# Five interleaved seven-product groups per chunk instead of three groups and six plain units, in a fused sliding-window attention and SwiGLU kernel

## The chip, the cores and the metric

One core of a Trainium2 chip. The metric is the device time of one launch in microseconds (us). The kernel before took 318.54 to 323.70 us over all rounds, a spread of 1.6%, so each kernel was run several times, in rounds that also ran the kernel before on the same chip. Some executions are in a slower state, with a lower granted clock. Four runs are marked so (two of run 2, one each of runs 3 and 7); the text says so there. All others, and all profiled ones, were fast.

## The reference, cut to what matters

```python
# q, k, v: (8 batches, 8 heads, 576, 64), fp32
scores = q @ k.T / 8, only where |i - j| <= 32
x = (softmax(scores) @ v) as 4608 tokens x 512
out = (silu(x @ w_gate) * (x @ w_val)) @ w_out      # 512 -> 1536 -> 512
```

The FFN is nearly all of the work. It is done in nine chunks of 512 tokens; the attention for chunk j + 1 runs among the FFN matmuls of chunk j. Chunk 0 is set-up. Chunks 1 to 6 carry attention, chunk 7 only the rest of it, chunk 8 none.

## The kernel before, the parts that matter

A *unit* computes 128 columns of h = silu(gate) * val plainly: eight matmuls of 512 columns, one ScalarE operation and one VectorE operation. A *group* computes 256 columns of h for the 512 tokens with seven products in place of eight (Winograd's form of a 2 x 2 block product): 28 matmuls of 256 columns. Around them ScalarE has five operations (three copies and two silu) and VectorE four (three sums and the product of silu and val). Matmuls write to PSUM, here in eight *banks*; to *drain* a bank is to read its result out with VectorE or ScalarE, after which it is free.

```python
def group_steps(j, f, xs, banks): ...   # one group; X, Y, Z are PSUM tiles
    "P1": X = wv(0).b11        "s1": keep X (ScalarE)
    "P2": Y = wv(1).b21        "c11": val = Y + s1 (VectorE)
    "P5": Z = s1w.xs[0]        "p5": keep Z
    "P6": X += s2w.xs[1]       "u2": keep X
    "P7": X += s3w.xs[2]       "c22": gate = X + p5 (VectorE)    "sc": silu(gate)
    "P3": Z += s4w.b22         "c12": val = Z + u2 (VectorE)
    "P4": X += wg(1).xs[3]     "sd": silu(X)                     "hm": h = silu * val
    # (shown in short; the signs are in the sums of weights and of x)
```

The order in which the steps are issued is a list, and each engine works through its own part of it in order (`pg`, `pv`: the gate and val halves of a unit; `As`, `Ds`, `Bs`: sums of h, which the second half needs). First half of a chunk before the change (`pg`, `pv`: the gate and val halves of a unit; `As`, `Ds`, `Bs`: sums of h, which the second half needs):

```python
pg0 pva0 pvm0 q0 k0 q1 t0
1P1 1s1 pvb0 1P2 1P5 1p5 1P6 1c11 1u2 pg1 ...
...
3P1 3s1 ... 3P7 3P3 3c22 m2 pvn3 3c12 3sc s3 3P4 m3 3sd
pg4 3hm pv4 s4 t6 m4 Bs0 flag pg5 pv5 s5 m5 Bs1 Bs2
```

Note the last line: after the last group's last product `3P4` two whole units follow, sixteen 512-column matmuls. The second half of a chunk (again seven products, now over h, here p1 to p7) with the attention of the next chunk in it:

```python
st["p1"](); st["s1"]()
...                                    # the rest of the sums of h, on VectorE
scores(0, ps_c); scores(1); scores(2)
exp(0); exp(1); exp(2)
st["p2"](); st["c11"]()                # c11: an output sum on VectorE
masked(0); masked(1); masked(2)        # VectorE
st["p6"](); st["u2"](); st["p5"](); st["k5"]()
av(0); av(1, ps_a); av(2, ps_a)        # attention x values
norm(0); norm(1); norm(2)              # VectorE; then the token transpose by DMA
st["p7"]() ...
```

The chain behind `norm` matters later: norm, DMA transpose of x into xT (the input of the next chunk's first matmul), and in the same queue the ten transposes of the q and k tokens that the scores half a chunk later need.

Of the kernel before, what the change touches and what calls it, by code (L numbers as in the profile page):

```python
# [132 lines left out]
def kernel(  # L133
# [29 lines left out]
    qk16 = fast.enter_context(tc.tile_pool(name="qk16", bufs=4))  # L163
    tkpool = fast.enter_context(tc.tile_pool(name="tk", bufs=18))
# [6 lines left out]
    ps_a = fast.enter_context(tc.tile_pool(name="ps_a", bufs=2, space=bass.MemoryType.PSUM))  # L171
    ps_c = fast.enter_context(tc.tile_pool(name="ps_c", bufs=1, space=bass.MemoryType.PSUM))
    ps_o = fast.enter_context(tc.tile_pool(name="ps_o", bufs=2, space=bass.MemoryType.PSUM))
# [102 lines left out]

    def cast_qk(st, cast):
        t16 = qk16.tile([128, J9, 2, D], FP16, tag="qk16", name="t16")
        cast(t16.rearrange("p j h d -> p h j d"),
             st.rearrange("p h (j d) -> p h j d", d=D))  # L280
        return t16
# [15 lines left out]


    xts = {}
# [24 lines left out]
    def pair_scores(m, pool=None, masked=True):  # L324
        s = (pool or ps_a).tile([128, 2, 8, 64], FP32, tag="c" if pool is ps_c else "a",
                                name="s_ps")
        for i in range(2):
            for g in range(HP):
                score_mms(s, 4 * i + g, m, i, g)
        p = pts[m] = ppool.tile([128, 2, 2, HP, 64], FP16, tag="p", name="p_t")  # L330
        ex = lambda: exp_act(p.rearrange("p e i g q -> p (e i g) q"),
                             s.rearrange("p e c q -> p (e c) q"))
        if not masked:
            return ex
        ex()
        pair_mask(m)

    def quad_scores(ms, F):

        if ms not in quads:  # L340
            quads[ms] = ppool.tile([128, 2, 2, 2, HP, 64], FP16, tag="p2", name="p2_t", bufs=2)
            for n, m in enumerate(ms):
                pts[m] = quads[ms][:, n]
# [19 lines left out]
    def pair_av(m, pool=None, normed=True):  # L363
# [3 lines left out]
        else:  # L367
            t2 = (pool or ps_c).tile([128, 2, 512], FP32, tag="a" if pool is ps_a else "c",
                                     name="o_ps")
# [30 lines left out]
    def turn_x(ms, pool, cast=None):  # L400
# [6 lines left out]
        if pool is None:  # L407
# [3 lines left out]
                       tag={ps_a: "a", ps_c: "c", ps_o: "o"}[pool], name="xt_ps")  # L411
# [4 lines left out]
        cast(dst.rearrange("p g (n t) -> p n g t", t=128), tp)  # L416
# [38 lines left out]
    def group_weights():  # L455

        s3 = qkst.tile([128, 3, 2, 768], FP16, tag="qkst", name="g_top")
        s4 = const.tile([128, 2, 768], FP16, name="g_rest")
        half = lambda w, k: w[:, 2 * k:2 * k + 2].rearrange(
            "p k (a c) -> p k a c", c=512)[:, :, :, 0:256]  # L460
        v0, v1, g0, g1 = half(wv16, 0), half(wv16, 1), half(wg16, 0), half(wg16, 1)
        gw["s"] = [s3[:, 0], s3[:, 1], s3[:, 2], s4]
        t1, t2, t3, t4 = [t.rearrange("p k (a c) -> p k a c", c=256) for t in gw["s"]]
        return [lambda k=k, o=o, a=a, b=b, op=op:
                nc.vector.tensor_tensor(out=o[:, k], in0=a[:, k], in1=b[:, k], op=op)
                for o, a, b, op in ((t1, g0, g1, ALU.add), (t2, t1, v0, ALU.subtract),
                                    (t3, v0, g0, ALU.subtract), (t4, v1, t2, ALU.subtract))
                for k in range(2)]

    def group_steps(j, i, xs, tiles):  # L470

        f = 2 * i
        x = xts[j]
        b11, b21, b22 = x[:, 0:2, 0:256], x[:, 2:4, 0:256], x[:, 2:4, 256:512]
        wv = lambda k: wv16[:, 2 * k:2 * k + 2, 512 * i:512 * i + 256]
        wg = lambda k: wg16[:, 2 * k:2 * k + 2, 512 * i:512 * i + 256]
        s1, s2, s3, s4 = [t[:, :, 256 * i:256 * i + 256] for t in gw["s"]]
        k = {}
        first = "ZX" if i == 2 else "X"

        def product(name, lhs, rhs, first):
            for n in range(2):
                for g in range(2):
                    nc.tensor.matmul(out=k[name][:, n], lhsT=lhs[:, g, 128 * n:128 * n + 128],  # L484
                                     rhs=rhs[:, g, :], start=(first and n == 0 and g == 0),
                                     stop=(g == 1), skip_group_check=True)

        def bank(name):
            pool = tiles[name]
            t = pool.tile([128, 2, 256], FP32, tag="c" if pool is ps_c else "o",  # L490
                          name=f"g{name}_ps")
            k[name] = t

        def keep_act(name, src):
            k[name] = opool.tile([128, 2, 256], FP32, tag="kept", name="kept", bufs=3)
            cast_act(k[name], k[src])

        def val(c, src, name):
            if "val" not in k:
                k["val"] = qk16.tile([128, 2, 512], FP16, tag="qk16", name="val")  # L500
            nc.vector.tensor_tensor(out=k["val"][:, :, 256 * c:256 * c + 256], in0=k[src],  # L501
                                    in1=k[name], op=ALU.add)
# [5 lines left out]
        def silu(c, src):  # L508
            if "silu" not in k:
                k["silu"] = qk16.tile([128, 2, 512], FP16, tag="qk16", name="silu")  # L510
            nc.scalar.activation(out=k["silu"][:, :, 256 * c:256 * c + 256], in_=k[src],  # L511
                                 func=AF.Silu, bias=0.0, scale=1.0)

        return {
            "P1": lambda: ([bank(n) for n in first], product("X", wv(0), b11, True)),
            "s1": lambda: keep_act("s1", "X"),
            "P2": lambda: (bank("Y"), product("Y", wv(1), b21, True)),
            "c11": lambda: val(0, "Y", "s1"),
            "P5": lambda: ("Z" in k or bank("Z"), product("Z", s1, xs[0], True)),
            "p5": lambda: keep_act("p5", "Z"),  # L520
            "P6": lambda: product("X", s2, xs[1], False),
            "u2": lambda: keep_act("u2", "X"),
            "P7": lambda: product("X", s3, xs[2], False),
            "c22": gate,
            "sc": lambda: silu(1, "gate"),
            "P3": lambda: product("Z", s4, b22, False),
            "c12": lambda: val(1, "Z", "u2"),
            "P4": lambda: product("X", wg(1), xs[3], False),
            "sd": lambda: silu(0, "X"),
            "hm": lambda: nc.vector.tensor_tensor(out=hts[j][:, 2 * f:2 * f + 2, :],  # L530
                                                  in0=k["silu"], in1=k["val"], op=ALU.mult),
        }

    def x_sums(j, eng):

        x = xts[j]
        b11, b12 = x[:, 0:2, 0:256], x[:, 0:2, 256:512]
        b21, b22 = x[:, 2:4, 0:256], x[:, 2:4, 256:512]
        t = ppool.tile([128, 4, 2, 256], FP16, tag="p2", name="x_sums", bufs=2)
        t1, t2, t3, t4 = [t[:, n] for n in range(4)]  # L540
        for o, a, b in ((t1, b12, b11), (t2, b22, t1), (t3, b22, b12), (t4, b21, t2)):
            eng.tensor_tensor(out=o, in0=a, in1=b, op=ALU.subtract)  # L542
        return t1, t2, t3, t4

    def unit_steps(j, fk):
# [3 lines left out]
        def half(i, w, parts=None):  # L549
            if i == 0:  # L550
                k["gv"] = ps_a.tile([128, 2, 512], FP32, tag="a", name="gv_ps")
            for g, c in parts or [(g, slice(0, 512)) for g in range(GS)]:
                nc.tensor.matmul(out=k["gv"][:, i, c], lhsT=w[:, g, 128 * fk:128 * fk + 128],  # L553
                                 rhs=xts[j][:, g, c], start=(g == 0 and c.start == 0),
                                 stop=(g == GS - 1), skip_group_check=True)

        def silu():
            k["s"] = spool.tile([128, 512], FP16, tag="s", name="ssb")
            nc.scalar.activation(out=k["s"], in_=k["gv"][:, 0, :], func=AF.Silu, bias=0.0,  # L559
                                 scale=1.0)  # L560

        first, second = [(0, slice(0, 256))], [(0, slice(256, 512))]
        most = [(g, slice(0, 512)) for g in range(1, GS)]
        return {"pg": lambda: half(0, wg16), "pv": lambda: half(1, wv16), "s": silu,
                "pva": lambda: half(1, wv16, first), "pvb": lambda: half(1, wv16, second),
                "pvm": lambda: half(1, wv16, most), "pvn": lambda: half(1, wv16, most + second),
                "m": lambda: nc.vector.tensor_tensor(out=hts[j][:, fk, :], in0=k["s"],  # L567
                                                     in1=k["gv"][:, 1, :], op=ALU.mult)}
# [3 lines left out]
    def wino_weights():  # L572
# [3 lines left out]
        rest = qkst.tile([128, 2, FKS // 2, 256], FP16, tag="qkst", name="ws_rest")  # L576
# [12 lines left out]
    def wino_sums(j, lo, hi, eng=None):  # L589

        h = hts[j].rearrange("p (f c) q -> p f c q", c=2)[:, lo:hi]
        a11, a21 = h[:, :, 0, 0:256], h[:, :, 0, 256:512]
        a12, a22 = h[:, :, 1, 0:256], h[:, :, 1, 256:512]
        s1, s2, s3, s4 = [t[:, lo:hi] for t in ws["s"]]
        tt = lambda o, a, b, op: (eng or nc.vector).tensor_tensor(out=o, in0=a, in1=b, op=op)  # L595
        return [lambda: tt(s1, a21, a22, ALU.add), lambda: tt(s2, s1, a11, ALU.subtract),
                lambda: tt(s3, a11, a21, ALU.subtract), lambda: tt(s4, a12, s2, ALU.subtract)]

    def wino_steps(j, split):
# [4 lines left out]
        (s1, s2, s3, s4), (t1, t2, t3, t4) = ws["s"], ws["t"]  # L604
        if split:
            x = [ps_c.tile([128, 256], FP32, tag="c", name="x_ps"),
                 ps_a.tile([128, 256], FP32, tag="a", name="x_ps")]
            y = [ps_o.tile([128, 256], FP32, tag="o", name="y_ps") for _ in range(2)]
            z = []
            parts = (0, 1)  # L610
        else:
            xt = ps_o.tile([128, 2, 256], FP32, tag="o", name="x_ps")
            yt = ps_o.tile([128, 2, 256], FP32, tag="o", name="y_ps")
# [379 lines left out]
```

## Time and profile before

| | us |
|---|---|
| median of the three runs known before the prediction | 322.83 (320.06 to 323.7) |
| profiled span | 317.8 |
| chunk 1, 2, ... 8 (from the first unit matmul of one to that of the next) | 32.07, 32.50, 32.00, 32.28, 31.77, 32.30, 29.30, 29.25 |

The chunk lengths are read from the timeline of TensorE. The prediction below shows and reads the page, the work by stage and the chain.

### The profile page before, as it was taken

What the parts mean: (1) busy time and instruction counts of PE and PEld (TensorE: products, weight loads), DVE (VectorE), ACT (ScalarE), POOL (GpSimd) and SP (SyncE); (2) the same over time, 40 slices, a digit from 0 to 9 for tenths busy, and PEclk for the clock granted to TensorE, in tenths of its full rate; (3) what the DMA queues carried; (4) which work ended last, traced back from release to release, by engine and by line L of the source; (5) the groups of instructions that cost most, each with busy time, mean ns of one, the idle gap of its engine ahead of it and who ended that gap; (6) DMA issues with size and microseconds to landing.
All of it is one profiled execution on the core that took longest, in us unless ns stands there. A gap on an engine that the chain in (4) does not pass through costs nothing.

```text
span 317.8 us, 8145 instructions
## 1 busy us (share of the span) xinstructions
PE 303.6 (96%) x3220; PEld 213.2 (67%) x3220; DVE 219.1 (69%) x404; ACT 192.7 (61%) x309; POOL 182.4 (57%) x231
## 2 busy tenths in 40 slices
PE   5779999999999999999999999999999999999991
PEld 3444555676877687768776877677767776777581
DVE  2654398788866787678757885887588958737760
ACT  3774559665756575667466846684668566336530
POOL 8973678649358934994489339953440538303300
PEclk9999999999999999999999999999999999999997
DMA  7999999999959996999799989999651330030012
GB/s 274 166 192 296 244 179 177 200 143 165 158 136 128 172 163 142 121 183 152 164 132 161 159 171 124 136 175 163 153 127 42 95 92 3 24 110 0 0 51 92
DMA packets 155916, 44.22 MB, mean 139 GB/s; under 512 B 136416, under 2 KB 153312, under 8 KB 155872
## 3 DMA queue, kind: packets, MB, share of 16 engines
q0 software_dynamic: 100640, 16.52, 79.3%
q1 hardware_dynamic: 55232, 27.11, 40.7%
q8 instruction: 27, 0.44, 0.6%
q14 instruction: 17, 0.14, 0.2%
HBM read 37.75 MB, written 9.44 MB: 148 GB/s over the span
## 4 chain that ended last, share of the span: by engine, by line
PE 88%; DVE 4%; DMA 3%; ACT 2%; issue 1%; SPq 0%; ACTq 0%
PE gv_ps L553 26%; PE gX_ps L484 13%; PE x_ps L627 12%; PE y_ps L627 9%; PE gZ_ps L484 7%; PE gv_ps L427 6%; PE o_ps L374 4%; PE gY_ps L484 3%; PE ob L441 3%; PE s_ps L312 3%; DMA qk_st<-in_k_dram 3%; PE xt_ps L414 1%; DVE s_top L595 1%; PE z_ps L627 1%; DVE p_t L358 1%
## 5 line engine op out<-in xcount | busy, mean ns | idle before, releaser
L553 PE MATMUL gv_ps<-xT,wv 128*128 128x512 f16 (+1 forms) x224 | 57.2, 349 | 0.0
L553 PE MATMUL gv_ps<-xT,wg 128*128 128x512 f16 x192 | 49.4, 379 | 0.0
L542 POOL TENSOR_TENSOR x_sums<-xT 128x512 f16<-128x512 f16 x14 | 17.4, 1246 | 49.1 <-DVE xT L271 29.3
L595 POOL TENSOR_TENSOR s_top<-hT 128x256 f16<-128x256 f16 x32 | 21.6, 674 | 40.1 <-PE gY_ps L484 28.8
L318 ACT ACTIVATE p_t<-s_ps 128x1024 f16<-128x1024 f32 (+1 forms) x40 | 34.7, 924 | 14.2 <-PE s_ps L312 14.2
L268 ACT ACTIVATE kept<-gX_ps 128x512 f32<-128x512 f32 x48 | 28.6, 595 | 18.1 <-PE gX_ps L484 18.1
L567 DVE TENSOR_TENSOR hT<-ssb,gv_ps 128x512 f16<-128x512 f16 x48 | 32.7, 682 | 9.9 <-ACT ssb L559 9.9
L559 ACT ACTIVATE ssb<-gv_ps 128x512 f16<-128x512 f32 x48 | 28.6, 596 | 17.1 <-PE gv_ps L553 17.1
L506 DVE TENSOR_TENSOR gate<-gX_ps,kept 128x512 f32<-128x512 f32 x24 | 16.6, 692 | 25.9 <-PE gX_ps L484 17.0
L553 PEld LDWEIGHTS <-wv 128*128 128x128 f16 x224 | 21.9, 98 | 17.9
L484 PEld LDWEIGHTS <-g_top 128*128 128x128 f16 x288 | 27.5, 98 | 6.6 <-ACT kept L268 1.5
L627 PEld LDWEIGHTS <-hT 128*128 128x128 f16 x288 | 27.4, 98 | 5.3 <-issue 0.3
L627 PEld LDWEIGHTS <-s_top 128*128 128x128 f16 x288 | 27.7, 98 | 4.1 <-issue 0.6
L511 ACT ACTIVATE silu<-gate 128x512 f16<-128x512 f32 x24 | 15.1, 630 | 24.5 <-DVE gate L506 24.5
L484 PE MATMUL gX_ps<-x_sums,g_top 128*128 128x256 f16 x192 | 28.8, 273 | 0.0
L553 PEld LDWEIGHTS <-wg 128*128 128x128 f16 x192 | 17.6, 98 | 14.6
L501 DVE TENSOR_TENSOR val<-gY_ps,kept 128x512 f16<-128x512 f32 x24 | 16.5, 687 | 14.8 <-ACT kept L268 13.6
L223 POOL DMA_DIRECT2D tok<-in_q_dram x30 | 25.8, 860 | 1.1 <-DMA wo<-in_moe_w_out_dram 1.1
L223 POOL DMA_DIRECT2D tok<-in_k_dram x30 | 25.9, 862 | 0.5 <-DMA wo<-in_moe_w_out_dram 0.5
L392 DVE TENSOR_TENSOR x<-o_ps,rall 128x512 f16<-128x512 f32 x36 | 24.9, 691 | 1.2
L627 PE MATMUL x_ps<-w_top,s_top 128*128 128x256 f16 x192 | 23.6, 273 | 0.0
L322 DVE TENSOR_TENSOR p_t<-p_t,mask 128x1024 f16<-128x1024 f16 x32 | 21.4, 705 | 1.8 <-ACT p_t L318 1.1
(114 smaller groups left out, 618.4 us busy)
## 6 DMA issues: line engine op xcount, KB each, us to landing
out_dram<-osb SPq DMA_DIRECT2D x32, 256.0 KB, 3.1
v<-v SPq DMA_DIRECT2D x12, 264.0 KB, 5.7
v<-in_v_dram POOLq DMA_DIRECT2D x24, 128.0 KB, 7.1
tok<-in_q_dram POOLq DMA_DIRECT2D x24, 128.0 KB, 6.3
tok<-in_k_dram POOLq DMA_DIRECT2D x24, 128.0 KB, 6.5
qk_st<-in_q_dram SPq DMA_DIRECT2D x4, 576.0 KB, 6.9
qk_st<-in_k_dram SPq DMA_DIRECT2D x4, 576.0 KB, 9.1
v<-in_v_dram POOLq DMA_DIRECT2D x16, 96.0 KB, 6.7
```

The lines of the kernel that those rows point to most:

```text
L223: nc.gpsimd.dma_start(out=t[0:n].rearrange("p (h d) -> p h d", d=D), in_=src[b].rearrange("h s d -> s h d")[128 * m:128 * m + n])
L268: nc.scalar.activation(out=o, in_=i, func=AF.Copy, bias=0.0, scale=1.0)
L318: nc.scalar.activation(out=o, in_=s, func=AF.Exp, bias=0.0, scale=1.0 / float(D) ** 0.5)
L322: nc.vector.tensor_tensor(out=flat, in0=flat, in1=mask, op=ALU.mult)
L392: nc.vector.tensor_tensor(out=x16s[m][:, a], in0=ov[:, :, :, 0:D], in1=r.unsqueeze(3).to_broadcast([128, a.stop - a.start, 4, D]), op=ALU. ...
L427: nc.tensor.matmul(out=gv[:, i, :], lhsT=w[:, g, 128 * fk:128 * fk + 128], rhs=xts[j][:, g, :], start=(g == 0), stop=(g == GS - 1))
L484: nc.tensor.matmul(out=k[name][:, n], lhsT=lhs[:, g, 128 * n:128 * n + 128], rhs=rhs[:, g, :], start=(first and n == 0 and g == 0), stop=( ...
L553: nc.tensor.matmul(out=k["gv"][:, i, c], lhsT=w[:, g, 128 * fk:128 * fk + 128], rhs=xts[j][:, g, c], start=(g == 0 and c.start == 0), stop ...
L559: nc.scalar.activation(out=k["s"], in_=k["gv"][:, 0, :], func=AF.Silu, bias=0.0, scale=1.0)
L567: "m": lambda: nc.vector.tensor_tensor(out=hts[j][:, fk, :], in0=k["s"], in1=k["gv"][:, 1, :], op=ALU.mult)}
L595: tt = lambda o, a, b, op: (eng or nc.vector).tensor_tensor(out=o, in0=a, in1=b, op=op)
L627: nc.tensor.matmul(out=dst[n], lhsT=lhs[:, f, 128 * n:128 * n + 128], rhs=rhs[:, f, :], start=(first and f == 0 and (split or n == 0)), st ...
```

## The change

Its intent: turn four of the six plain units of each chunk into two more groups (0.4 us of matmul columns less for each), interleave the groups in eight single PSUM banks with an order list tuned for each kind of chunk, split the sums of h between VectorE and GpSimd block by block, and put the sums of x on GpSimd ahead of the token loads. Its core, with cuts:

```diff
-    ORDER = """
-        pg0 pva0 pvm0 q0 k0 q1 t0
-        1P1 1s1 pvb0 1P2 1P5 1p5 1P6 1c11 1u2 pg1 pva1 s0 k1 check t1 t2 1P7 1P3 1c22 ...
-        ...
-        pg4 3hm pv4 s4 t6 m4 Bs0 flag pg5 pv5 s5 m5 Bs1 Bs2
-    """
+    ORDER = {                  # step@bank/engine; groups 0 to 4, units 50 and 51; S = sums of h
+        "first": """ ... """,
+        "even": """
+            u50v0@3 u50g0@2 T3/D av@4@5 T1/G u50g1 u50v1 n0 u50s u50m 1P1@6 T2/G 0P1@0 1P5@7 1s1
+            ...
+            4c22 ld7 3P3 3c12 u51g0@1 3sd 3sc u51g1 4P4 ld8 3hm S32/D 4sc 4P2@6 S03/G 4P3 u51s S30/G
+            4sd S20/D u51v0@7 4c11 u51v1 4c12 tabE S22/G u51m ld9 S31/D sc12@0@1@2@3 sc0@4@5 ex2 4h0
+            ex0 S50/G 4h1 F1a@6 F1 S21/D S40/D S51/G S23/D k2 F2@7 S41/G Fs1 k0 ex1 k1 S52/G Fc11
+            S33/D S13/D S42/D F6 av012@4@5@0@1@2@3 Fu2 F5 m0 S53/D m1 Fk5 m2 F7 sc34@4@5@0@1 S43/D
+            ...
+        """,
+        "odd": ..., "seven": ..., "last": ...
-    t = ppool.tile([128, 4, 2, 256], FP16, tag="p2", name="x_sums", bufs=2)
+    t = ppool.tile([128, 4, 2, 256], FP16, tag="x_sums", name="x_sums", bufs=1)
-    k["gv"] = ps_a.tile([128, 2, 512], FP32, tag="a", name="gv_ps")
+    k[i] = bank.tile([128, 512], FP32, tag="b", name="gv_ps")          # single banks
+def wino_sum(j, p, n, eng):                                            # one sum of h, one block
+    eng.tensor_tensor(out=o, in0=a, in1=b, op=op)
```

In the new list `sc` are scores, `ex` exponentials, `k` masks, `av012` attention x values, `m` norms, `F` the second half's products, `ld` token loads.

## The prediction

> **What bounds the kernel now.** I read the page first (engine shares, slices, chain), then the busy time by stage, then the chain in order of time, and last TensorE's timeline of one chunk. Page, engine shares, two rows of the slices, and the chain by engine:
>
> ```profile
> PE 303.6 (96%) x3220; PEld 213.2 (67%) x3220; DVE 219.1 (69%) x404; ACT 192.7 (61%) x309; POOL 182.4 (57%) x231
> ...
> PE   5779999999999999999999999999999999999991
> ...
> PEclk9999999999999999999999999999999999999997
> ...
> PE 88%; DVE 4%; DMA 3%; ACT 2%; issue 1%; SPq 0%; ACTq 0%
> ```
>
> TensorE is busy in 96% of the span at the full clock and carries 88% of the chain. A busy matmul engine may still be slow inside its busy time, so the next view is the work by stage. The stages are chunk 3 and chunk 4 (the first two lines), then chunks 7 and 8, which have little or no attention left:
>
> ```profile
> 124.28:156.29 32.01, 32.01 (x358) 23.70 (x358) 23.95 (x44) 20.22 (x34) 22.41 (x28) 1.00 1.58 148
> 156.29:188.56 32.27, 32.27 (x385) 23.95 (x386) 23.80 (x44) 21.37 (x35) 21.41 (x27) 1.00 1.67 156
> 252.64:282.04 29.40, 28.98 (x222) 21.37 (x222) 19.04 (x34) 13.53 (x25) 13.27 (x15) 1.00 0.18 54
> 282.04:312.00 29.96, 29.20 (x222) 21.13 (x220) 18.60 (x38) 15.29 (x30) 5.51 (x8) 1.00 0.13 45
> ```
>
> Columns: stretch, its length, then busy time of PE, weight loads, DVE, ACT, POOL. TensorE has no idle time in a middle chunk; DVE has about 8 us of it, ACT about 11. The rates are in the chain in order of time (start, length, what):
>
> ```profile
> 75.97 3.45 PE gv_ps L553 x16
> 79.43 1.31 PE x_ps L627 x12
> ...
> 97.86 0.87 PE gX_ps L484 x8
> ...
> 249.09 0.69 DVE osb L656
> 249.81 0.97 ACT p_t L318
> 250.80 1.35 DVE p_t L322
> ...
> 271.98 1.02 DVE s_top L595
> ...
> 275.98 0.61 DVE osb L656
> 276.64 1.47 PE y_ps L627 x12
> ```
>
> A 512-column matmul advances the engine by 3.45/16 = 215.6 ns, a 256-column one by 1.31/12 = 109.2 ns (the group products, 0.87/8, the same). The 273 and 379 ns of the groups' means are latencies that overlap, not costs. From these rates a chunk's FFN is: six plain units of eight 512-column matmuls, 48 x 215.6 = 10.35 us; three seven-product groups of 28 matmuls, 84 x 109.1 = 9.16 us; the second FFN, 84 more, 9.17 us; together 28.7 us. Four or five attention pairs (0.81 us of scores and 0.90 us of attention x values for each three) add 2.3 to 2.9 us, the transposes 0.45 us, and each of four attention blocks a chunk costs another 0.1 us around it (the next product then takes 1.42 instead of 1.31 us in the chain), 0.4 us. That gives 31.9 to 32.5 against chunks of 31.8 to 32.5 us: the chunk is matmul columns and nothing else. The true waits of the steady part are few: about 0.25 us at the end of chunk 6 (the DVE, ACT, DVE lines at 249 to 252 us) and 0.6 us in chunk 7, where a product at 276.64 waits for an output sum that queued behind DVE's sums of h.
>
> **What the Trainium skill says.** (1) "TensorE: Matmul & The Clock Gate", section "Back-to-back issue gap", gives N/2.4 + 2.5 ns for a warm matmul of N columns: 215.8 and 109.2 ns. The trace agrees to 0.1 ns, so columns are the cost and halving a matmul costs only the fixed 2.5 ns. (2) "SBUF — State Buffer", section "SBUF: two separate sides": a GpSimd operation and a VectorE operation with two SBUF inputs exclude each other for a whole instruction. The trace agrees: the product of silu and val (two SBUF inputs) takes 679 to 1089 ns, while the unit's product, with one input in PSUM, never exceeds 689 ns. The same shows here:
>
> ```profile
> 136.25 1.09 DVE L530 TENSOR_TENSOR hT<-silu,val 128x1024 f16<-128x1024 f16 x1 [0.21 <-ACT silu L511]
> 141.42 0.68 DVE L530 TENSOR_TENSOR hT<-silu,val 128x1024 f16<-128x1024 f16 x1
> ```
>
> (3) "PSUM — Partial Sum Buffer", section "The four PSUM rules": one matmul's output fits one bank of 512 fp32. A group's product of 2 x 256 fills exactly one of eight, which is why eight single banks let several groups be open together.
>
> **The change, part by part.** *Columns.* In each of eight chunks two groups replace four plain units. Two units are 16 matmuls of 512, 3.45 us; one group is 28 of 256, 28 x 109.1 = 3.055 us. The saving is 0.395 us a group, 0.79 us a chunk, 16 x 0.395 = 6.3 us in all. It lies wholly on the bounding engine.
>
> *Drains.* DVE back to back advances about 0.60 us per 512-element PSUM operation (129.37, 129.98, 130.58 in its timeline), and its recorded 0.69 overlaps. A unit costs DVE one operation and ACT one; a group costs DVE four and ACT five. Two groups for four units: DVE +4 x 0.60 = +2.4 us a chunk, ACT +6 x about 0.55 = +3.3 us. Sums of h: all of blocks 2 to 5 were on DVE (four of 768 at 0.48 us and four of 256 at 0.21 us, 2.8 us); now 10 to 15 of the 24 single-block sums are DVE's, at 0.21 us, 2.1 to 3.2 us. One to four sums of x come to DVE at 0.36 us. DVE's dense work in a middle chunk is then: groups 20 x 0.60 = 12, units 1.2, output sums 1.8, masks 2.8, norms 4.5 x 0.84 = 3.8, sums 3.5, one transpose copy 0.6, sum 25.7 us of some 31.4, or 82%. Exclusion from GpSimd adds an estimated 25 two-input operations x a one in three chance x 0.35 us = 3 us: 91%. ACT goes from 20.2 to 21.4 to about 24 us, 77%. Neither becomes the bound on average.
>
> *GpSimd.* Four sums of x at 1.15 us and eight of h at 0.67 become one to three of x and 9 to 14 of h: 10.0 to about 9.5 us. Token loads (0.9 us of descriptor work each) still wait behind the sums of x, as before.
>
> *Waits removed.* Sums block by block, and the first product of the second FFN taking block 4 last, should close chunk 7's 0.6 us, and chunk 6's 0.25. In chunk 0 the sums of weights start four units earlier, so their end (0.94 us of two sums ahead of the copy to kT) shrinks by about 0.3 us. About 0.2 in the last chunk. Sum 1.3 us.
>
> *Added on the path.* In two odd chunks scores are taken in two places, one change more each way, 2 x 0.2 = 0.4 us. The fillers between the products of a group were plain units; now they are other groups, which themselves need drains. At the end of a chunk's first FFN, the fifth group must pass P4, silu, the product with val and the sums while TensorE has only one half unit, scores and ten matmuls, some 2.7 us, to cover DVE work of about 2.5 us. I allow 0.2 us of new wait a chunk, 1.7 us in all. Net: 6.3 + 1.3 - 0.4 - 1.7 = 5.5 us.
>
> **The rivals.** *A, DVE becomes the bound at the turn to the second FFN.* For it: 91% on average, in-order queues, fewer units to hide behind, longer two-input operations. Against: 8 us of slack now, and an order list so fine that it must have been tuned on drain times. At 0.8 us lost per chunk the column saving is eaten: 321 to 323 us. *B, clean fit.* No new waits and all 1.3 us recovered: 6.3 + 1.3 - 0.4 = 7.2 us, 315.6 us, 2.2%. For it: the present order leaves PE no idle time at all in five chunks, so such fits are possible. *C, late tokens or values.* One token buffer fewer, and x sums ahead of the loads, could make scores late. Against: no PE wait in the chunks is on a DMA, loads land in 6 to 7 us, and they are used a chunk later. If it held: one or two us. *D, PSUM re-layout, twice a chunk.* New tiles wait for the last readers of other shapes. The norms and score drains precede by 2 us or more, so I give it 0.1 us a chunk, inside the allowance.
>
> **Range and chances.** From the median before, 322.83 - 5.5 = 317.3 us, 1.7% less. The runs before spread from 320.06 to 323.7, so a run alone is uncertain by about 1.5 us either way. Low end: clean fit from a low run (320.06 - 7.2 = 312.9), taken a little less extreme, 314. High end: the gain falls to about 2 us, 321. Faster by over 2% needs 6.5 us, more than the columns alone give, so it needs almost the clean fit: 0.28. Within 2%: 0.68. Slower by over 2% would need new waits of 13 us: 0.04.
>
> **What would show it.** The 512-column unit matmuls should drop to a third per chunk, 48 to 16; group matmuls rise from 84 to 140 a chunk, still stepping by 109 ns. Middle chunks should last 31.0 to 31.7 us. Chunk 7 should lose more, about 1.4 us. DVE should be busy 27 to 30 us in a middle chunk, with more sums at 0.5 us and over. Right: the list of waits shows PE or its weight loads waiting on DVE for under 2 us in all. Wrong, by rival A: such waits total 4 us or more, gathered before the products of the second FFN, released by sums or products of h. Wrong, by C: waits of scores on a DMA. If the span falls by over 7 us, the allowance for new waits was the error.

## The result, and the profile after

| | before | after |
|---|---|---|
| median, same rounds, us | 321.44 (319.27 to 323.70, 4 runs) | 334.65 (333.11 to 337.03, 4 runs) |
| profiled span, us | 317.8 | 331.4 |
| chunk 1 | 32.07 | 36.56 |
| chunk 2 | 32.50 | 35.18 |
| chunk 3 | 32.00 | 33.20 |
| chunk 4 | 32.28 | 35.67 |
| chunk 5 | 31.77 | 34.29 |
| chunk 6 | 32.30 | 32.73 |
| chunk 7 | 29.30 | 29.27 |
| chunk 8 | 29.25 | 28.41 |

The ratio is 1.0417, 95% interval 1.0306 to 1.0527: slower by 4%. Here and below a ratio is the mean time of one kernel's fast runs over that of the kernel before's fast runs of the same rounds, so it is not quite the ratio of the medians; for the experiments below it leaves the profiled run out, while the time given is the median of all runs. The measured median lies 13.7 us above the top of the predicted range, 321 us.

The page of the changed kernel:

```profile
PE 303.4 (92%) x3380; PEld 230.5 (70%) x3380; DVE 260.6 (79%) x501; ACT 217.7 (66%) x358; POOL 194.3 (59%) x245
...
PE   5789999898899998998999879989999999999991
...
PE 1%; ACT 0%; issue 0%
```

Busy time of TensorE is as before, 303 us, though fewer columns are computed: part of the lost time lies inside what is counted as busy. Its slices have dropped from an unbroken row of nines to eights and sevens. The last line is the chain by engine, and it is a warning: it breaks off after 1% of the span at a step with no releaser, so on this kernel the chain of waits tells nothing and the timeline has to be read instead.

The work by stage of the changed kernel (stretch, length, busy time of PE, weight loads, DVE, ACT, POOL, then the granted clock); the stretches lie within about 1 us of chunks 2, 3, 5 and 8:

```profile
94.00:129.50 35.50, 33.67 (x405) 27.11 (x402) 30.86 (x57) 25.22 (x42) 23.42 (x29) 1.00 1.72 149
129.50:163.00 33.50, 31.60 (x387) 25.67 (x388) 27.00 (x56) 22.99 (x39) 24.20 (x27) 1.00 1.51 147
...
199.20:233.50 34.30, 33.15 (x388) 26.60 (x389) 26.83 (x57) 22.87 (x38) 24.33 (x28) 0.95 1.46 142
...
295.50:324.00 28.50, 28.39 (x244) 23.29 (x242) 22.92 (x50) 17.57 (x35) 8.04 (x12) 1.00 0.14 48
```

TensorE now idles 1.2 to 1.9 us in the three chunks with attention, where before it idled nowhere. VectorE is at 27.0 to 30.9 us (27.3 to 29.9 between the exact starts of chunks 2 to 5), the 27 to 30 that the prediction gave. No engine is full.

**Gained against lost.** I took the starts of all matmuls from 57 us on, and for each kind of matmul (line and columns) the median step to the next one. The sum of these median steps is what the columns cost; what is over it is lost time. Columns: 246.2 us before, 240.1 after, 6.1 us less; the FFN's kinds alone fell by 6.5 us (6.3 were predicted). Lost: 7.8 us before, 26.6 after (a few matmuls missing from a trace make both a little rough; of the 7.8, 3.9 are steps between attention matmuls, which come in short and long ones). So 18.8 us of new lost time took the columns' gain back: net 12.7 us, against 13.2 us between the medians.

**Where the waits are.** From the timeline of TensorE after the change, lines of chunks 1 to 3 and of the start of chunk 5 (start, length, what, and in brackets the idle time before it and what ended it):

```profile
62.41 1.03 PE L509 MATMUL gX_ps<-xT,wv 128*128 128x256 f16 x8 [1.41 <-DVE hT L594]
...
77.30 0.60 PE L509 MATMUL gX_ps<-x_sums,wg 128*128 128x256 f16 x4 [0.77 <-DVE gate L526]
...
121.17 0.45 PE L385 MATMUL o_ps<-v,p_t 128*64 128x66 f16 x16 [0.57 <-DVE p_t L333]
...
130.38 0.60 PE L583 MATMUL gv_ps<-xT,wg 128*128 128x512 f16 x2 [1.43 <-DMA xT<-x]
...
151.84 0.29 PE L323 MATMUL s_ps<-qT,kT 64*128 64x64 f16 x8 [0.90 <-DMA kT<-tok]
...
199.25 0.61 PE L583 MATMUL gv_ps<-xT,wg 128*128 128x512 f16 x2 [2.13 <-DMA xT<-x]
...
201.23 1.03 PE L583 MATMUL gv_ps<-xT,wg 128*128 128x512 f16 x2
202.06 1.06 PE L583 MATMUL gv_ps<-xT,wv 128*128 128x512 f16 x2
```

They fall into three sets. In chunk 1 a first product waits for a bank that the unit ahead of it still holds (1.41 us), and two last products wait for their gate (77.30, and 0.87 us at 79.20). In even chunks (115.96, shown below, and 121.17) scores wait for a bank that the last group's `val` has not left, and attention x values wait for the masks. At the start of chunks 3 and 5 the first matmul waits for xT by DMA, and later in them scores wait for kT by DMA. The last two lines show an added cost after the longest such wait: two 512-column matmuls advance the engine by 0.83 us (201.23 to 202.06) where they took 0.43 us, which is the 0.95 of the clock in the table of chunk 5. The granted clock is half for 3.41 us there (from 200.27 us), which costs 1.7 us. Six of the 17 traces have one such stretch, some of them in set-up, so a chunk of a single trace can be 1.7 us longer for this alone.

The totals by cause (us in all, times, longest):

```profile
PE gv_ps L583 <- DMA xT<-x: 3.6, 2, 2.1
...
PE o_ps L385 <- DVE p_t L333: 2.7, 8, 0.6
PE s_ps L323 <- DMA kT<-tok: 2.0, 2, 1.1
```

With scores on `val` (1.5 us in chunks 2, 4 and 6) and, in chunk 1, the gates (1.6), the bank (1.4) and an output sum (0.8), that is 13.6 us: 5.6 on transfers, 4.2 on masks and `val`, 3.8 in chunk 1. The half clock adds 1.7. The rest of the 26.6 us, about 11, is short steps that no wait explains, against about 7 before.

**The turn between the halves.** What TensorE does around the end of the first half in chunk 2, before the change (`gX` with `wg` is the last product of the last group, `x_ps<-wo,hT` the first of the second half):

```profile
107.38 0.60 PE L484 MATMUL gX_ps<-x_sums,wg 128*128 128x256 f16 x4
107.81 1.03 PE L553 MATMUL gv_ps<-xT,wg 128*128 128x512 f16 x4
...
111.27 1.47 PE L627 MATMUL x_ps<-wo,hT 128*128 128x256 f16 x12
112.67 0.87 PE L312 MATMUL s_ps<-qT,kT 64*128 64x64 f16 x48
```

and after it:

```profile
112.37 0.60 PE L509 MATMUL gX_ps<-x_sums,wg 128*128 128x256 f16 x4
...
113.83 1.03 PE L583 MATMUL gv_ps<-xT,wv 128*128 128x512 f16 x4
114.79 0.64 PE L323 MATMUL s_ps<-qT,kT 64*128 64x64 f16 x32
115.96 0.41 PE L323 MATMUL s_ps<-qT,kT 64*128 64x64 f16 x16 [0.53 <-DVE val L521]
```

Before, two whole units lie between the last group product and the second half: 111.27 - 107.81 = 3.46 us in which VectorE drains the last group. After, half a unit does (0.86 us) beside the group's own remaining products. The units that became groups were the cover of the turn. On VectorE, the same stretch before (the output sum, three masks, the first norm):

```profile
115.07 0.69 DVE L656 TENSOR_TENSOR osb<-y_ps,kept 128x512 f32<-128x512 f32 x1
115.68 1.88 DVE L322 TENSOR_TENSOR p_t<-p_t,mask 128x1024 f16<-128x1024 f16 x3
118.03 0.21 DVE L391 RECIPROCAL rall<-o_ps 128x8 f32<-128x8 f32 x1 [0.47 <-PE o_ps L374]
```

and after (halves of the product of silu and val, three masks, the first norm):

```profile
116.63 1.71 DVE L535 TENSOR_TENSOR hT<-silu,val 128x512 f16<-128x512 f16 x2
...
118.87 2.85 DVE L333 TENSOR_TENSOR p_t<-p_t,mask 128x1024 f16<-128x1024 f16 x3
...
122.85 0.20 DVE L402 RECIPROCAL rall<-o_ps 128x8 f32<-128x8 f32 x1
```

VectorE has no idle time from 109 to 129 us. The masks start 4.1 us after the first scores (118.87 - 114.79) instead of 3.0 (115.68 - 112.67), three of them take 2.85 us instead of 1.88, and the first norm comes 8.1 us after the scores instead of 5.4. The lengthened operations are those with two SBUF inputs, while GpSimd works on sums of h in the same stretch. The DMA transpose of x can only follow the norm. Its issue, before and after:

```profile
118.99 1.25 SPq L408 DMA_TRANSPOSE xT<-x  x1
...
123.80 1.21 SPq L419 DMA_TRANSPOSE xT<-x  x1
```

It is issued 9.0 us after the first scores instead of 6.3, and it lands 6.5 us later (at 130.33) instead of 3.2 (at 122.18). Late issue and slow landing together are the 1.43 us at 130.38. The one that chunk 5 waits for takes 7.0 us to land (issued at 192.18), 5.0 before the change.

### The profile page after: what moved, and what is told of

It is laid out like the page before.

```text
span 331.4 us, 8641 instructions
## 1 busy us (share of the span) xinstructions
PE 303.4 (92%) x3380; PEld 230.5 (70%) x3380; DVE 260.6 (79%) x501; ACT 217.7 (66%) x358; POOL 194.3 (59%) x245
## 5 line engine op out<-in xcount | busy, mean ns | idle before, releaser
L624 POOL TENSOR_TENSOR s_top<-hT 128x256 f16<-128x256 f16 x48 | 37.6, 800 | 57.2 <-DVE hT L535 42.7
L273 ACT ACTIVATE kept<-gX_ps 128x512 f32<-128x512 f32 x80 | 45.7, 598 | 11.5 <-PE gX_ps L509 9.2
L535 DVE TENSOR_TENSOR hT<-silu,val 128x1024 f16<-128x1024 f16 (+1 forms) x48 | 34.1, 724 | 1.2 <-ACT silu L531 0.4
L526 DVE TENSOR_TENSOR gate<-gX_ps,kept 128x512 f32<-128x512 f32 x40 | 27.5, 687 | 8.7 <-ACT kept L273 5.1
L653 PEld LDWEIGHTS <-s_top 128*128 128x128 f16 x288 | 27.3, 98 | 5.2 <-issue 0.8
L521 DVE TENSOR_TENSOR val<-gZ_ps,kept 128x512 f16<-128x512 f32 x40 | 27.2, 684 | 0.9 <-PE gZ_ps L509 0.4
L509 PEld LDWEIGHTS <-g_more 128*128 128x128 f16 x256 | 25.1, 98 | 3.3
L273 ACT ACTIVATE kept<-gZ_ps 128x512 f32<-128x512 f32 x40 | 23.9, 598 | 3.1 <-PE gZ_ps L509 2.9
L531 ACT ACTIVATE silu<-gX_ps 128x512 f16<-128x512 f32 x40 | 23.9, 598 | 2.9 <-PE gX_ps L509 2.3
L509 PE MATMUL gX_ps<-x_sums,wg 128*128 128x256 f16 x160 | 24.0, 272 | 1.6 <-DVE gate L526 1.6
L624 POOL TENSOR_TENSOR s_top<-s_top,hT 128x256 f16<-128x256 f16 x23 | 18.9, 828 | 9.4 <-DVE s_top L624 9.1
```

Source lines behind the costliest of these rows:

```text
L273: nc.scalar.activation(out=o, in_=i, func=AF.Copy, bias=0.0, scale=1.0)
L509: nc.tensor.matmul(out=k[name][:, n], lhsT=lhs[:, g, 128 * n:128 * n + 128], rhs=rhs[:, g, :], start=(pool is not None and n == 0 and g == 0),
L521: nc.vector.tensor_tensor(out=k["val"][:, :, cols(c)], in0=k[src], in1=k[name], op=ALU.add)
L526: nc.vector.tensor_tensor(out=k["gate"], in0=k["X"], in1=k["p5"], op=ALU.add)
L531: nc.scalar.activation(out=k["silu"][:, :, cols(c)], in_=k[src], func=AF.Silu, bias=0.0, scale=1.0)
L535: nc.vector.tensor_tensor(out=hts[j][:, 2 * f:2 * f + 2, c], in0=k["silu"][:, :, c], in1=k["val"][:, :, c], op=ALU.mult)
```

## The experiments

Theories that could explain the 18.8 us. The queue of VectorE at the turn (D): too much work on it, in the wrong order, with too few matmuls to cover it. Sums on GpSimd (G): they lengthen VectorE's two-input operations and delay the value loads. Transfers (X): the DMA turns of x and of the tokens come late by themselves. Order of the norms at the start of a chunk (Q). Where the expectations use a letter, it is one of these. "The change" below has the ratio 1.0417.

**1. All sums of h on VectorE.** Every `S../G` in the list becomes `S../D`, nothing else.

```diff
-            4P6 3c22 2P3 2P4 2c12 4P5@5 S00/G 2sc 4u2 3P4 S10/D S02/G 2sd S11/D 4P7 4p5 2hm S01/G
+            4P6 3c22 2P3 2P4 2c12 4P5@5 S00/D 2sc 4u2 3P4 S10/D S02/D 2sd S11/D 4P7 4p5 2hm S01/D
```

> All 24 block sums of h a chunk on VectorE, none on GpSimd. Theory D (VectorE's queue is full at the turn to the second FFN): VectorE gets 9 to 14 more sums of 0.21 us, about 2.3 us a chunk, so waits for masks and scores grow and the time rises from 334.6 by 4 to 12 us. Theory G (the sums on GpSimd do the harm: they lock VectorE's two-input operations out, hold VectorE up where one sum needs another engine's sum, and push the loads of v onto the transposes of x): VectorE operations stop reaching 0.9 us and over, the loads of v issue some 5 us earlier, and the time falls by 4 to 9 us.

Measured: 328.95 us, ratio 1.0247 (1.0167 to 1.0326). Putting *more* operations on VectorE made the kernel 1.6% faster than the change (1.0247 over 1.0417; all four runs, 326.9 to 331.5, lie under the change's lowest, 333.11). So the split between the engines does harm, and the number of operations on VectorE alone is not the bound. By which of theory G's three ways it does harm, this run does not separate. It does not bring the kernel back: scores in chunk 5 now wait 2.78 us for kT.

**2. Values loaded early.** The first four value slabs of the next chunk are issued right after the last token load, ahead of the late sums on GpSimd.

```diff
-            load_v(b, range(5))
+            load_v(b, range(5) if j == 2 else (4,))
...
+                if not loads and b + 1 > 3:
+                    load_v(b + 1, range(4))
```

> The loads of v for the next chunk, except the last slab, are issued right after the last token load, ahead of the late sums on GpSimd; nothing else moves. Theory X (the waits at the start of chunks 3 and 5 come from DMA traffic of v that meets the transpose of x): that transpose lands in about 3 us in place of 6.5, both waits and the half clock after the second go, the time falls by 4 to 6 us. Theory D (the norm is late because VectorE is late): the transpose is issued as late as now, and the time falls by less than 2 us.

Measured: 334.03 us, ratio 1.0414 (1.0327 to 1.0501). Two of the four runs are marked slow (335.95 and 337.32), and one of them is in the ratio; the fast ones are 329.98 and 332.11, 1.0323 times the kernel before. So the gain is unclear, between none and about 1%. The trace, of a fast run, is clearer: the same transposes land in 3.3 and 3.8 us in place of 6.5 and 7.0, TensorE's waits for xT are gone and so is the half clock. The value loads did slow these transfers. But the loads now stand ahead of GpSimd's sums, and TensorE waits 5.2 us in all for those. In its timeline:

```profile
120.50 0.28 PE L653 MATMUL x_ps<-w_top,s_top 128*128 128x256 f16 x1 [1.78 <-POOL s_top L624]
```

What was waited for at the chunk's start is now waited for at its turn.

**3. The first pair of chunks 3 and 5 turned on TensorE** instead of by the DMA.

```diff
-    URGENT = {1: (1, 2), 2: (1, 2), 3: (0, 1), 4: (1,), 5: (0,)}
+    URGENT = {1: (1, 2), 2: (0, 1, 2), 3: (0, 1), 4: (0, 1), 5: (0,)}
```

> In chunks 2 and 4 the first pair's x is turned on TensorE with the others instead of by the DMA. It costs TensorE 4 x 56 ns and VectorE about 0.2 us a chunk. The waits of 1.6 and 2.3 us at the start of chunks 3 and 5, and about 1.9 us of matmuls at half clock after the second, go whatever made the transpose late: the time falls by 4 to 6 us, unless VectorE's own copy is then late (theory D in its strong form): under 2 us.

Measured: 330.16 us, ratio 1.0317 (1.0262 to 1.0373), 1% faster than the change (1.5% without the run marked slow, 332.49). Chunk 5 falls from 34.29 to 32.65 us, where the half clock (1.7 us) is gone too, and chunk 2 from 35.18 to 33.82. The late xT is a real part of the loss, a quarter to a third of it.

**4 and 5. No masks, in the change and in the kernel before** (wrong results; a relative error of 0.74 in both). In the change this takes some 20 us of work (DVE 260.6 to 239.3) off VectorE.

```diff
-            steps[f"k{i}"] = lambda i=i: pair_mask(todo[i])
+            steps[f"k{i}"] = lambda: None
```

> Wrong result on purpose: the multiplication by the mask is left out in chunks 1 to 6 (4 or 5 operations of 0.63 us and over a chunk on VectorE, and the wait of attention x values on them). Theory D: the waits of about 1.1 us before attention x values in chunks 2, 4 and 6 go, norms come 2 to 4 us earlier, so the waits for x go as well: the time falls by 8 to 12 us. Theory G or X alone: 2 to 4 us.

> Control, wrong result on purpose: the kernel before, without the masks of chunks 1 to 6, as they were left out of the changed kernel. There VectorE has about 8 us of slack a chunk and TensorE has no waits to remove but 0.25 us at the end of chunk 6. If the earlier gain of 2.3% from leaving the masks out was VectorE's queue: no change here, within 0.3% of 320.5 us. If masks cost time in any kernel: 3 to 6 us less.

Measured: the change without masks 326.33 us, ratio 1.0184 (1.0139 to 1.0229), 2.2% faster than with them; the kernel before without masks 320.10 us, ratio 1.0035 (0.9962 to 1.0108), no difference. The same work is free in one kernel and costs 7 us in the other. So VectorE's queue is on the path after the change and was not before it. Some 44% of the loss (0.0184 of 0.0417) stays without masks, so this isn't all of it.

**6. Norms of the carried pairs first.** At the start of each chunk, norms move ahead of the first sums of x.

```diff
-            u50v0@3 u50g0@2 T3/D av@4@5 T1/G u50g1 u50v1 n0 u50s u50m 1P1@6 ...
+            av@4@5 n0 u50v0@3 u50g0@2 T3/D T1/G u50g1 u50v1 u50s u50m 1P1@6 ...
```

> The changed kernel with one move: each chunk begins with the carried pairs' attention x values and their norms, so the transposes of x, q and k, which the queue of SyncE takes one after the other behind the norms, begin 1.5 to 3 us earlier. Theory Q (that chain, norm, then 10 transposes in order, then landing, about 20 us, is as long as the shortened first FFN, so scores wait for k at the end of chunks 3 and 5): those waits of 1.0 to 1.3 us go, the time falls by 2 to 5 us. Theory D alone (VectorE's queue at the turn): less than 1 us.

Measured: 333.75 us, ratio 1.0401 (1.0323 to 1.0480): no gain as a whole. Chunk 7 falls from 29.27 to 28.09 us, the 1.2 us that had been missing there, but chunk 2 grows to 37.05: the next chunk's first matmul now waits 3.00 us for xT (1.43 in the change).

**7. All repairs together**: 1, 3 and 6, and in chunk 1 other banks for the products that waited and the sums of weights moved.

```diff
-            ... u50s T2/D u50m 0P1@1 W0 0s1 1P1@0 W1
+            ... u50s T2/D u50m 0P1@7 W0 0s1 1P1@5 W1
```

> Five groups kept, and all repairs together: sums of h on VectorE, the first pair of chunks 2 and 4 turned on TensorE, norms first, and in chunk 1 other PSUM banks for the first products and the weight sums moved off the second FFN. If GpSimd's sums, the transposes and the order made the loss: 315 to 321 us, at or under the kernel before. If the fifth and fourth group's own drains on VectorE are the bound (theory D): 323 to 327 us, with waits of scores and products on VectorE left.

Measured: 326.97 us (326.72 without the run marked slow, 331.15), ratio 1.0202 (1.0132 to 1.0273). Taking 1.6% and 1% off the change would by themselves give about 326 us, so within the noise runs 1 and 3 account for all of it, and the rest of the repairs shows no gain. In chunk 3 the scores now stop for kT for 1.25 us. Shorter first halves bring the scores forward, and the transposes behind the norms do not come forward with them. In the kernel before, the fourth of five k transposes is issued at 138.07 us, lands at 143.02, and the scores start at 145.18: only 2.2 us between landing and use. That path was nearly as long as TensorE's all along, without showing as a wait.

**8 and 9. Four groups and four units, with all repairs.** In 8 the second added unit's product stood behind the scores that needed its bank, so scores waited up to 1.65 us in each of chunks 2 to 6. That is a fault of my list. In 9 it stands ahead of them.

```diff
-        for f in range(5):
+        for f in range(4):
-        for c in range(2):
+        for c in range(4):
...
-            ... 4P1@3 ... 4c22 ... 4P4 ... 4h0 ... 4h1 ...
+            ... u52g0@3 ... u53g0@2 u53g1 ... u52s u53s u53m u52m ...
```

> The same repairs with four groups and four plain units in place of five and two: 0.4 us more of matmul columns a chunk (3.2 us in all), but per chunk 1.2 us less on VectorE (two operations) and 1.6 us less on ScalarE (three). Theory D: faster than the kernel of five groups with all repairs by 1 us or more. Otherwise slower than it by about 3 us.

> All repairs together, with four groups instead of five in each chunk (the fifth group becomes two plain units), and the second unit's product placed ahead of the first's so that the scores of the carried attention don't wait for its bank, which spoilt the run before this one. If the fifth group's extra drains (four VectorE and five ScalarE operations against two and two) are what overloads the turn between the two halves, this should be faster than the all-repairs kernel (326.97 us) in spite of 3.1 us more of matmul columns: about 322 to 325 us. If instead the turn of tokens by DMA holds the odd chunks, whatever the number of groups, the extra columns partly hide in those waits and the time stays at 326 to 328 us. Over 330 us would say that the order of the list, not the amount of drain work, is what costs.

Measured: 331.87 us, ratio 1.0375 (1.0320 to 1.0431), and 328.34 us, ratio 1.0262 (1.0219 to 1.0305). Fewer drains, but not faster than five groups with the same repairs. One step in the wrong place cost 3.5 us (8 against 9). Taking drain work away did not help by itself. The time is just over the 326 to 328 us expected for the transfers, but the waits for xT and kT are gone from the trace, so that reading does not hold either.

**10. A mix.** Chunks 1 to 6 get a new list with four groups, the order of the second half as in the kernel before (scores right after the first product, masks behind the first output sum), and the sums of h of the last groups on VectorE; chunks 7 and 8 keep the change's five groups, with norms first.

```diff
-        name = {1: "first", NCH - 2: "seven", NCH - 1: "last"}.get(j, ("even", "odd")[j % 2])
+        name = {NCH - 2: "seven", NCH - 1: "last"}.get(j, "mid")
+        "mid": """ ... 2P4 2sd u53m 2hm 4P4 4sd tabE 4h0 4h1 S30/D ... F1a@6 F1 Fs1 sc0@4@5 sc12@0@1@2@3 ... """
```

> A mix: chunks 1 to 6, those with attention, take four groups, with the order of the second half of the chunk as in the kernel before (scores right after the first product, masks behind the first output sum, sums of h of the last groups on VectorE) and the norms of carried pairs first; chunks 7 and 8, which carry little attention, keep the five groups of the change. My theory (the change is right where VectorE has slack and wrong where masks, norms and sums meet at the turn) says 316 to 320 us: 0.4 us of columns in each of six chunks and 1.5 to 2 us in the last two, less some small waits, against 320 us of the kernel before. The rival, that interleaved groups in single banks lose by their layout and order wherever attention runs, whatever the load, says 323 us or more. Chunks 7 and 8 should last about 28.2 us each (29.3 before).

Measured: 327.72 us, ratio 1.0225 (1.0195 to 1.0255), 8 us over the range expected. Chunks 7 and 8 do about what was expected, 28.11 and 28.41 us, and the waits for xT and kT are gone, but the turn now waits for the last group's h in each of six chunks:

```profile
150.84 0.39 PE L653 MATMUL x_ps<-wo,hT 128*128 128x256 f16 x2 [1.15 <-DVE hT L535]
```

**11. The mix with a longer covered turn.** The same work, but a whole plain unit and one pair's scores now lie between the last group product and the end of the first product of the second half. (Other lines of the list, the sums of weights among them, move too.)

```diff
-            4P4 4sd tabE 4h0 4h1 S30/D S20/D S40/D S31/D
-            F1a@6 F1 Fs1 sc0@4@5 sc12@0@1@2@3 ...
+            4P4 4sd 4h0 4h1 u53g0@2 u53g1 S20/D S21/D u53v0@3 u53v1 u53s tabE S40/D S41/D u53m S30/D S31/D
+            F1a@6 sc0@4@5 F1 Fs1 sc12@0@1@2@3 ...
```

> The mix of the run before (four groups in chunks 1 to 6, five in 7 and 8), with one thing mended that its trace shows: the first product of the second half waited 1.31 us in each of six chunks for the last group's h, and a unit 0.41 us for its bank. Now a whole plain unit (eight 512-column matmuls, 1.72 us) and one pair's scores follow the last group's last product, and the first product takes the last two blocks at its end. If the length of covered time after the last group's last product is what decides the turn between the halves, both waits go, 1.72 us in each of six chunks, 10.3 us: about 317.5 us, against 327.7 us of the mix before it and 320.2 us of the kernel before the change; the middle chunks last 31.7 to 32.0 us. If VectorE's load or the turn of tokens holds the chunks, the waits move elsewhere and the time stays at 322 us or more.

Measured: 325.44 us, ratio 1.0143 (1.0104 to 1.0181). The wait for the last group's h is gone, but of the 10 us expected only 2.3 came: in five chunks the third pair's scores now stop, because the last unit's product stands on VectorE behind four sums that nothing needs yet. First the scores on TensorE, then VectorE's queue:

```profile
150.83 0.41 PE L323 MATMUL s_ps<-qT,kT 64*128 64x64 f16 x16 [0.85 <-DVE hT L594]
```

```profile
149.05 0.28 DVE L624 TENSOR_TENSOR s_top<-hT 128x256 f16<-128x256 f16 x1
...
150.10 0.68 DVE L594 TENSOR_TENSOR hT<-ssb,gv_ps 128x512 f16<-128x512 f16 x1
```

Its inputs had been ready since 147.9 us (ScalarE's silu ended at 147.65, the unit's last matmul at 147.88); it ran at 150.10.

**12. Five groups in an order of my own**, with scores, masks and norms as in the mix, half a unit and one pair's scores at the turn.

```diff
+        "mid": """ ... 4P4 4sd u51v0@1 u51v1 u51s tabE S30/D 4h0 4h1 u51m S40/D S50/D
+            sc0@4@5 F1a@6 F1 Fs1 sc12@0@1@2@3 ... """
```

> The five groups of the change in every chunk, but in my own order of the middle chunks: half a plain unit and one pair's scores after the last group's last product, the first product of the second half taking the two last blocks at its end, the scores, masks and norms placed as in the kernel before. VectorE's work in a chunk is that of the change, some 28 us of about 31.5. If it is the load on VectorE that decides, this stays near the repaired change, 324 to 330 us. If it is only the order at the turn, five groups should be worth 0.4 us a chunk more than four and give about 315 to 318 us.

Measured: 332.43 us, ratio 1.0348 (1.0316 to 1.0380). Five groups lost again: in each of chunks 2 to 5 four waits of 0.28 to 0.73 us, two last products on their gate, one on ScalarE's kept sums, and scores on VectorE. This was a first list, not a tuned one. Whether five groups can be had in these chunks without loss stays open.

**13. The mix of 11 with VectorE's queue reordered.** The last unit's product goes ahead of the four sums; in chunk 1 sums of weights go later. No work is added or taken away.

```diff
-            ... u53g0@2 u53g1 S20/D S21/D u53v0@3 u53v1 u53s tabE S40/D S41/D u53m S30/D S31/D
+            ... u53g0@2 u53g1 u53v0@3 u53v1 u53s tabE u53m S20/D S21/D S40/D S41/D S30/D S31/D W4
```

> The mix with the longer covered tail, with one order on VectorE mended: the trace of the run before shows the third pair's scores waiting 0.85 us (1.0 us lost) in each of five chunks for the last unit's product, which stood in VectorE's queue behind four sums of h that nobody needed yet; and in chunk 1 two waits of 0.84 and 0.60 us behind sums of weights. Now that product goes ahead of the sums and the sums of weights go later. No work is taken away, so if the order of VectorE's queue at the turn is the cause, 5 x 1.0 + about 1.4 us go: 319 us, against 325.4 us of the run before and 320.5 us of the kernel before the change. If the load is the cause, the queue only hands the wait on and the time stays above 323 us.

Measured: 321.86 us, ratio 1.0048 (0.9990 to 1.0106). Of the 6.4 us expected 3.6 came, from the order of VectorE's operations alone. The stops at the turn are gone. What is left is chunk 1 (two waits of 0.47 and 0.60 us for the gate) and, at the start of chunk 5, 0.84 us for xT by DMA.

**14. The same without masks** (wrong result, relative error 0.74).

```diff
-            steps[f"k{i}"] = lambda i=i: pair_mask(todo[i]) if i < n else None
+            steps[f"k{i}"] = lambda i=i: None
```

> The same kernel without the masks (a wrong result on purpose), the counterpart of the two runs without masks made earlier, where the change gained 2.3% and the kernel before nothing. If the tail is now long enough and in the right order, the masks are hidden and this gains under 0.5% on the same kernel with masks; if the turn is still bound by VectorE's load, it gains 1% or more.

Measured: 322.10 us, ratio 1.0031 (0.9981 to 1.0081): the masks cost nothing any more. VectorE's busy time, 250.0 us with masks and 234.7 without, is off the path again, as in the kernel before.

**15. The last visible waits mended**: chunk 1's sums of weights in a stretch where VectorE idles, two sums of h behind the masks, and run 3's turn on TensorE.

```diff
-            ... 1P6 1c11 1u2 ld3 ld4
+            ... 1P6 1c11 1u2 ld3 ld4 W2 W3 W4
-            S50/D S51/D S52/D S53/D S10/G ...
+            S50/D S51/D S10/G ...
-    URGENT = {1: (1, 2), 2: (1, 2), 3: (0, 1), 4: (1,), 5: (0,)}
+    URGENT = {1: (1, 2), 2: (0, 1, 2), 3: (0, 1), 4: (0, 1), 5: (0,)}
```

> The reordered mix with its last visible waits mended: in chunk 1 the sums of weights move to a stretch where VectorE idles 2.2 us (two waits of 0.47 and 0.60 us of TensorE on the gate there), two sums of h move behind the masks, and the first pair of chunks 3 and 5 is turned on TensorE instead of by the DMA (a wait of 0.84 us on that DMA, and 0.3 us in another chunk). If these waits are real losses, 1.3 + 1.2 us go: about 319.4 us, 0.4% under the kernel before (320.8). If the turn moves a wait to the tokens' transposes instead, as in the runs before, it stays at 321 to 322 us.

Measured: 320.49 us (320.17 to 320.76, six runs), ratio 0.9983 (0.9951 to 1.0015): the same as the kernel before, 4% under the change. Two of its stages, chunk 3 and most of chunk 4:

```profile
126.00:158.00 32.00, 32.00 (x381) 24.71 (x379) 27.27 (x57) 21.65 (x37) 23.54 (x27) 1.00 1.76 146
158.00:191.00 33.00, 32.73 (x385) 25.21 (x383) 26.41 (x55) 22.54 (x38) 23.08 (x28) 1.00 1.58 149
```

VectorE is at 27.3 us in 32 and 26.4 in 33, which is 85 and 80%, and TensorE hardly idles (0.27 us in the second line). In the change VectorE had 27 us in 33.5 and 31 us in 35.5, 81 and 87%, and TensorE did. By the count of steps the lost time is 10.4 us, against 7.8 before the change and 26.6 after it. This version does not beat the kernel before by a measurable amount. With four groups in six chunks and five in two it should save 6 x 0.4 + 2 x 0.8 = 4 us of columns, and the FFN's matmuls do step 4.1 us less in all; 2.6 us of lost time and the added turns on TensorE (0.7 us) give most of it back. It keeps the single banks, the two re-layouts of PSUM a chunk and the smaller buffers of the change, so these alone don't make the 4%.

## Why the prediction was wrong, point by point

- **Columns, 6.3 us: right.** The median steps are unchanged (216 ns and 109 ns), and the sum of the FFN's steps fell by 6.5 us. (The trace agrees with the page's formula to 0.2 ns, 215.6 against 215.8, not to 0.1.) In chunk 8, which has no attention, the gain shows in full: 0.84 us where 0.79 was predicted.
- **Work of VectorE, 27 to 30 us a middle chunk: right** (27.3 to 29.9 in chunks 2 to 5). The mean share did not decide: run 15 has about the same share (80 and 85%) and is 4% faster.
- **New waits, "I allow 0.2 us of new wait a chunk, 1.7 us in all": this is the step that failed.** The new lost time is 18.8 us. The prediction compared about 2.7 us of cover at the turn with about 2.5 us of VectorE's work. The work that really stands in the queue between the last group's gate (111.64 us in chunk 2) and the first mask (118.87) is 7.2 us without a gap: a gate, three vals, the products of silu and val, a unit's product and six sums of h. And the cover that the kernel before had there, two units of 3.46 us, is just what the change turned into groups. I listed the removed units as columns saved and did not ask what they covered.
- **Rival A, VectorE at the turn: the largest part by the runs, but not as written.** Without the masks 2.2 of the 4.2% go, though the waits that the trace puts down to masks and `val` are just 4.2 us: the late norms carry the delay on to xT. TensorE waits for VectorE at the turn in even chunks, but before scores and attention x values, released by `val` (a bank) and by masks, and not before the products of the second half, released by sums of h. The runs without masks (7 us in the change, nothing before it, nothing in the reordered mix) show that VectorE's queue is on the path, and 11 and 13 show that cover and order decide it.
- **Rival C, late transfers, dismissed because no PE wait was on a DMA: wrong.** The transfers are late twice over: the norms that release them come 2.7 us later after the scores, and they take 6.5 and 7.0 us to land in place of 3.2 and 5.0, because value loads behind late GpSimd sums fall into the same moment (in run 2, with the loads moved, 3.3 and 3.8 us). A path with no wait in the profile can still have hardly any slack, and I did not measure the slack. Waits of 1.4 and 2.1 us on xT, a half clock of 1.7 us after the second, and 0.9 to 1.1 us on kT came out of it, and run 3 got 1% or more back.
- **Rival D, the re-layout of PSUM, 0.1 us a chunk inside the allowance: too small.** In even chunks scores wait 0.53 us for a bank, and in chunk 1 a product waits 1.41 us.
- **The splitting of sums over two engines** was counted only as 3 us more of VectorE's busy time. As a delay on the path it cost 1.6% (run 1).
- **Chunk 7's gain of 1.4 us** did not come (0.03 us). With the norms first it did (1.2 us, run 6).

What stays open: the causes have no fixed shares. Runs 1, 3 and 4 gain 1.6, 1.0 and 2.2%, all repairs together 2.1%, within the noise of what 1 and 3 give; in several traces a wait that was taken away came back elsewhere (kT in runs 1 and 7, GpSimd's sums in run 2). About 4 of the 18.8 us are short steps that I can't put down to a wait. And a tuned list with five groups in the attention chunks was not found, nor ruled out.

## What to carry to other kernels

Before you replace work on the bounding engine by cheaper work, ask what the removed instructions covered: an engine that idles nowhere hides drains, and the last stretch before a dependency needs cover of its own. A mean share of 80 to 90% on the other engines says little; list what stands in their queue, in order, between the last producer and its first consumer. And a path that shows no wait still has a slack: compute it from issue, landing time and first use before you call it hidden.

## What the Trainium skill lacked or had wrong

- "SBUF — State Buffer", section "SBUF: two separate sides", has the exclusion of GpSimd and two-input VectorE operations, and the traces agree with it: three masks took 2.85 us while GpSimd worked on sums of h and 1.88 us otherwise. It warns that the second one to issue blocks; what neither it nor another page has is what a split of such sums costs a whole kernel: with every sum of h back on VectorE the kernel was 1.6% faster (ratio 1.0247 against 1.0417).
- "TensorE: Matmul & The Clock Gate", section "Part 1: The HAM clock gate (the "warmup" mystery)", gives an idle window of about 3.4 us before the clock is halved. Here a recorded wait of 2.13 us was followed by two 512-column matmuls in 0.83 us instead of 0.43 us. The half clock lasted 3.41 us, and in the 3.41 us before it TensorE idled about 2.4 us in all; in the other five traces with such a stretch that was 2.1 to 3.0 us (idle counted as a step's length over its kind's median; one stretch of run 2 with 2.1 us had none after it). The measurement decides: a window need not be wholly idle.
- No page that I found says how to find the slack of a path that shows no wait, or that the chain view can break off at a step without a releaser (here after 1% of the span).
